# Three-pass products for two more layers of the first block, and the order of the splits around them

## The chip, the cores and the metric

One Trainium2 chip, one of its cores. The metric is the device time of one execution in microseconds (us); for the kernel before it is the median of three runs.

## What is computed

The reference has three parts in a row. The first is a linear attention with decay over 4 sequences of 768 steps with 8 heads of 48 columns (`state` is a 48x48 matrix for each sequence and head). The second is a feed-forward layer pair 384 -> 2048 -> 384 with a clipped gate, the third a gated pair 384 -> 1536 -> 384 behind a root-mean-square norm:

```
y[t]  = r[t] @ (state + (u * k[t]) (x) v[t]);  state = w[t] * state + k[t] (x) v[t]
h = x @ w_in;   x = (h * clip(h + 3, 0, 6) / 6) @ w_out
xn = x / rms(x) * rms_g;   out = (silu(xn @ w_gate) * (xn @ w_val)) @ w_out
```

All inputs and outputs are float32. The change lies in the second part, at its first block of tokens, and in the hand-over of attention output to the second block.

## The kernel before, in words

**Blocks and steps.** The 768 positions are cut into six blocks of 128 positions of all 4 sequences (512 tokens each). For each block c the second part runs over 16 tiles f of 128 hidden columns. One pass over a tile is a step; `steps` numbers them. Block 0 has its first five tiles cut in two halves of 256 tokens (steps 0 to 9), then whole tiles (step n has tile f = n - 5, steps 10 to 20). Block 1 is steps 21 to 36 (f = n - 21).

**What a step issues.** In this order: the list `before[n]`; `ff1` (first product of this tile into one of two PSUM buffers `hps`, then the clip on ACT, L466, and the product with h on DVE, L467, which frees that buffer); the list `between[n]`; `ff2` of the tile two steps earlier (the second product); the list `behind[n]`. After each step `pin` chains the instructions of every engine, so that each engine takes them in exactly the order of the program. An instruction that waits holds up all that stand behind it on its engine.

**Two ways to multiply.** For block 0 and f below `F32_F` the products are plain float32: `emit_h_f32` and `emit_out_f32` (L455, L461), six matrix products for a layer half. From `F32_F` on, and in all later blocks, each operand is a pair of parts, a high one (a rounded copy made on ACT) and a low one (the rest, made by a subtraction), and `emit_h` and `emit_out` (L449, L478) make three passes over three slices, nine products. The split of the activation is `emit_split`: high part on ACT (L471), low part on POOL (L472). The split of the block's tokens is `x_parts` for block 0 (L608 on ACT, L609 on DVE) and `Job.split` for later blocks (L425 on ACT, L426 on POOL).

**Weights.** A tile of the second part's weights comes as 64-bit words: `load` (L138, SP), `scale` (L146, ACT), `bits` (L151, L152, DVE), which puts them into a tile `x`, and from there a transfer (L155, SP) to their place in `wide_a` or `wide_b`. `parts` (L161 on ACT, L162 on DVE) turns that into the high and low part. Steps: for f below 12 `parts` runs two steps before block 1 needs the tile (f + 19); for f from 12 on, one step before block 0 does (f + 4).

**Attention.** Each job j (block j // 4, sequence j % 4) is laid out by `plan(j, n)` over six steps: `scans` (two scans, L280, DVE) and `bonus1` (L307, L308, POOL) at n; `muls` (L303, DVE), `bonus2` (L312, DVE, a sum over what `bonus1` made) and `decay` (POOL) at n + 1; `fill` (eight copies, L338, ACT), `pe_a` (L361), `pe_kt` (L345), `choose` (L367, DVE), `copy_kt` (L350, ACT) at n + 2; `pe_y` (L397, L403), `pe_u` (L376), `copy_y` (L409 on ACT, then eight transfers by SP, L412 to L415), `add_u` (L385, DVE) at n + 3; `split` at n + 5. Jobs 4 to 7 have n = 6, 9, 12, 15, jobs 8 and 9 have n = 19 and 23. So `pe_y` of job 7 is in step 18, its `split` in step 20, and `pe_y` of job 8 is in step 22. Block 1's first product, step 21, reads the split of job 7; `choose` writes over the tile that `fill` wrote and `pe_y` multiplies by it.

Of the kernel before, what the change touches and what calls it, by code (L numbers as in the profile page):

```python
# [9 lines left out]
F32 = mybir.dt.float32  # L10
# [3 lines left out]
AF = mybir.ActivationFunctionType  # L14
ALU = mybir.AluOpType
AX = mybir.AxisListType

B, H, S, D = 4, 8, 768, 48
# [5 lines left out]
KT = DM // 128  # L24
F1 = 2048 // 128
# [4 lines left out]
WP = 4 * DM  # L30
NG = F2 // 3
LAGS = (5, 0, 0, 0, 0, 0)
F32_F = 12


@with_exitstack
def kernel(
# [15 lines left out]
    nc = tc.nc  # L53
# [23 lines left out]
    x0 = st_p.tile([128, KT, TOK], F32, tag="x0", name="x0", bufs=1)  # L77
# [53 lines left out]

    class Weight:
        def __init__(self, src):
            self.src, self.near = src, False

        def load(self):
            self.raw = st_p.tile([128, 2 * DM], U64, tag="raw", name="raw", bufs=3)
# [11 lines left out]
        def bits(self):  # L149
            x = st_p.tile([128, 2 * DM], U32, tag="x", name="x", bufs=3)  # L150
            nc.vector.tensor_scalar(x, self.words()[0], 29, None, ALU.logical_shift_right)  # L151
            nc.vector.scalar_tensor_tensor(  # L152
                out=x, in0=self.mag.bitcast(U32), scalar=3, in1=x, op0=ALU.logical_shift_left, op1=ALU.bitwise_or)
            self.x = x.bitcast(F32).rearrange("p (a n) -> p a n", a=2)
            nc.sync.dma_start(  # L155
                out=self.dst[:, :, 1, :].bitcast(U32), in_=x.rearrange("p (a n) -> p a n", a=2))
            if not self.near:
                self.x = self.dst[:, :, 1, :].bitcast(F32)
# [103 lines left out]
    xts = {0: xt_p.tile([128, KT, 2, TOK], F32R, tag="xt", name="xt")}  # L262
# [196 lines left out]
    def emit_out_f32(acc, slot, g, first, cols):  # L459
        for m in range(KT):  # L460
            nc.tensor.matmul(  # L461
                acc[m][:, cols], slot[:, m * 128:(m + 1) * 128], g,
                start=first, stop=True, skip_group_check=not first)
# [5 lines left out]
    def emit_split(a, n, p=None):  # L469
        g = (p or rg_p).tile([128, 2, n], F32R, tag="g", name="g")  # L470
        nc.scalar.activation(out=g[:, 0, :], in_=a, func=AF.Copy)  # L471
        nc.gpsimd.tensor_tensor(out=g[:, 1, :], in0=a, in1=g[:, 0, :].bitcast(F32), op=ALU.subtract)  # L472
        return g
# [9 lines left out]
    def new_acc():  # L483
        return [ps_o.tile([128, TOK], F32, tag=f"o{m}", name=f"o{m}") for m in range(KT)]
# [51 lines left out]
    wa = [Weight(wa_d[f]) for f in range(F1)]  # L536
# [9 lines left out]
    before, between, behind = ([[] for _ in steps] for _ in range(3))  # L546

    def plan(j, n):

        jb = jobs[j]  # L550
        before[n] += [jb.scans, jb.bonus1]
        before[n + 1] += [jb.muls, jb.bonus2, jb.decay]
        before[n + 2] += [jb.fill]
        between[n + 2] += [jb.pe_a, jb.pe_kt, jb.choose, jb.copy_kt]
        between[n + 3] += [jb.pe_y, jb.pe_u, jb.copy_y, jb.add_u]
        if j + 2 < len(jobs):
            behind[n + 3] += [lambda: jobs[j + 2].load("w", "rk", "v")]
        if j + 1 < len(jobs):
            behind[n + 1] += [lambda: jobs[j + 1].load("rks")]
        (before if jb.b == B - 1 else behind)[n + 5] += [jb.split]  # L560


    j0, j1, j2, j3 = jobs[:B]
# [11 lines left out]
    for j, n in zip(range(B, 2 * B), (6, 9, 12, 15)):  # L575
        plan(j, n)
    for c in range(2, NC_):
        for b in range(B):
            plan(c * B + b, first[c] - 18 + 4 * b)
# [6 lines left out]
        if f + 3 < F1:  # L586
            behind[n] += [wa[f + 3].load]
    for f in range(F1):
        if f in (6, 10):
            behind[f + 19] += [wa[f].parts]  # L590
        else:
            before[f + 19 if f < F32_F else f + LAGS[0] - 1] += [wa[f].parts]
    behind[2] += [lambda: jobs[4].load("w", "rk", "rks", "v")]
    behind[4] += [lambda: jobs[5].load("w", "rk", "v")]

# [6 lines left out]
    for c in range(1, NC_):  # L602
        norm_plan(c, first[c], False)

    def x_parts():
        for k in range(KT):
            h = xts[0][:, k, 0, :]
            nc.scalar.activation(out=h, in_=x0[:, k, :], func=AF.Copy)  # L608
            nc.vector.tensor_tensor(out=xts[0][:, k, 1, :], in0=x0[:, k, :], in1=h.bitcast(F32), op=ALU.subtract)  # L609

    behind[F32_F + LAGS[0] - 2] += [x_parts]
    acc, norms, todo = None, {}, []


# [12 lines left out]
    def ff1(c, f, cols):  # L627
        n = cols.stop - cols.start
        ps = ps_h.tile([128, n], F32, tag="h", name="hps")
        if c == 0 and f < F32_F:  # L630
            if cols.start:
# [4 lines left out]
        else:  # L636
# [3 lines left out]
            g = emit_split(a, n)  # L640
        x = wa[f].x[:, 1] if c == 0 and f < F32_F else wpair[f][:, 1]
        todo.append((c, f, cols, g, x))

    def ff2(c, f, cols, g, x):
        nonlocal acc
        first, last = f == 0 and cols.start == 0, f == F1 - 1
        if first:
            acc = new_acc()
        if c == 0 and f < F32_F:
            emit_out_f32(acc, x, g, first, cols)  # L650
# [5 lines left out]
    def run(fs):  # L656
        for x in fs:
            x()
# [302 lines left out]
    for i in range(2):  # L961
        nc.sync.dma_start(
            out=uc[64 * i:64 * i + D, :, i], in_=u_d.rearrange("o (p i d) -> i d (o p)", p=NP, i=2)[i])
# [24 lines left out]
    for f in range(W1):  # L988
        wa[f].dst = wpair[f]
        wa[f].near = f < 2  # L990
    run((j0.scans, j0.pairs, j0.pe_bonus, j0.muls, j1.pairs, j0.fill, j0.pe_a, wa[0].scale, j1.pe_bonus, j1.fill))
    run((j1.scans, j1.muls, lambda: j1.pe_a(True), j0.choose, j0.pe_y0, wa[0].bits, wa[3].load, j1.choose, j1.pe_y0))
    run((wa[1].scale, wa[1].bits, wa[4].load, j2.pairs, j2.scans, j0.copy_y0, j1.copy_y0))
# [150 lines left out]
    for j in range(6 * NG + 1):  # L1144
        p, k = divmod(j, 2 * NG)
# [34 lines left out]
        want, n = {5: 7, 6: 6}.get(j, 9), 0  # L1180
# [107 lines left out]
```

## Time and profile before

| | |
|---|---|
| median of 3 runs | 944.44 us (943.24 to 944.67) |
| the profiled execution | 943.37 us, of it 941.6 us from the first to the last instruction |
| TensorE (PE) busy | 926.5 us, 98%, granted clock 1.0 |
| VectorE (DVE) busy | 645.5 us, 69% |
| ScalarE (ACT) busy | 475.6 us, 51% |
| GpSimd (POOL) busy | 532.8 us, 57% |

An engine's busy share is an average over stages. Times in the rows below count from the first instruction of the execution. A row of the timeline merges equal instructions that follow each other; ends of matrix products are modelled and overlap the next one, so that the length of a stretch on PE is read from start to start. The bracket at the end of a row is the idle time of the engine just before it, with what ended it.

### The profile page before, as it was taken

What the parts mean: (1) busy time and instruction counts of PE and PEld (TensorE: products, weight loads), DVE (VectorE), ACT (ScalarE), POOL (GpSimd) and SP (SyncE); (2) the same over time, 40 slices, a digit from 0 to 9 for tenths busy, and PEclk for the clock granted to TensorE, in tenths of its full rate; (3) what the DMA queues carried; (4) which work ended last, traced back from release to release, by engine and by line L of the source; (5) the groups of instructions that cost most, each with busy time, mean ns of one, the idle gap of its engine ahead of it and who ended that gap; (6) DMA issues with size and microseconds to landing.
All of it is one profiled execution on the core that took longest, in us unless ns stands there. A gap on an engine that the chain in (4) does not pass through costs nothing.

```text
span 941.6 us, 14286 instructions
## 1 busy us (share of the span) xinstructions
PE 926.5 (98%) x5085; PEld 733.1 (78%) x5085; DVE 645.5 (69%) x913; ACT 475.6 (51%) x946; POOL 532.8 (57%) x454
## 2 busy tenths in 40 slices
PE   5999999999999999999999999999999999999998
PEld 5775578888878887777888888887877778888886
DVE  7787767776868777677545377648988467555555
ACT  4554656656545555654554654445555445433331
POOL 0033355766846776675466676589466678335423
PEclk9999999999999999999999999999999999999999
DMA  8888532247445554642653387763699732644321
GB/s 338 310 302 297 191 138 84 92 165 246 167 145 198 170 184 156 228 163 58 242 193 112 125 310 262 279 244 141 226 381 325 272 154 92 243 168 155 147 79 68
DMA packets 63127, 184.77 MB, mean 196 GB/s; under 512 B 8912, under 2 KB 23248, under 8 KB 58448
## 3 DMA queue, kind: packets, MB, share of 16 engines
q1 hardware_dynamic: 63056, 183.87, 55.1%
q8 instruction: 40, 0.66, 0.3%
q14 instruction: 31, 0.25, 0.1%
HBM read 134.29 MB, written 39.32 MB: 184 GB/s over the span
## 4 chain that ended last, share of the span: by engine, by line
PE 92%; DMA 3%; DVE 2%; ACT 1%; issue 1%; POOL 1%; SPq 0%; POOLq 0%; ACTq 0%
PE o L478 19%; PE hps L449 18%; PE o L765 15%; PE pe L765 10%; PE pc L765 9%; PE pa L765 4%; PE o L461 3%; PE hps L455 3%; PE pb L765 3%; PE aps L361 2%; PE yps L403 2%; DMA raw<-in_dram 2%; PE pd L765 1%; PE yps L397 1%; PE ktp L345 1%; PE ups L376 1%
## 5 line engine op out<-in xcount | busy, mean ns | idle before, releaser
L472 POOL TENSOR_TENSOR g<-a,g 128x512 fp32r<-128x512 f32 x84 | 115.9, 1379 | 145.0 <-ACT g L471 132.8
L467 DVE SCALAR_TENSOR_TENSOR a<-a,hps 128x512 f32<-128x512 f32 x84 | 57.3, 682 | 94.6 <-ACT a L466 93.1
L478 PE MATMUL o<-g,wide_b 128*128 128x512 f32 x441 | 113.3, 399 | 0.0
L449 PE MATMUL hps<-xt,wide_b 128*128 128x512 f32 x441 | 111.9, 398 | 0.0
L765 PE MATMUL o<-xt,wide_b 128*128 128x512 f32 x405 | 107.7, 395 | 0.0
L466 ACT ACTIVATE a<-hps,half 128x512 f32<-128x512 f32 x84 | 57.5, 684 | 94.3 <-PE hps L449 89.9
L449 PEld LDWEIGHTS hps<-xt,wide_b 128*128 128x128 f32 x441 | 82.7, 188 | 21.2 <-issue 1.2
L478 PEld LDWEIGHTS o<-g,wide_b 128*128 128x128 f32 x441 | 81.2, 188 | 19.4 <-issue 0.5
L471 ACT ACTIVATE g<-a 128x512 fp32r<-128x512 f32 x84 | 53.1, 633 | 78.9 <-DVE a L467 76.8
L765 PEld LDWEIGHTS o<-xt,wide_b 128*128 128x128 f32 x405 | 76.0, 188 | 18.3
L478 PE MATMUL o<-g,wide_a 128*128 128x512 f32 x315 | 78.7, 394 | 0.0
L449 PE MATMUL hps<-xt,wide_a 128*128 128x512 f32 x315 | 77.6, 390 | 0.2 <-POOL xt L426 0.2
L280 DVE TENSOR_TENSOR_SCAN w<-w,dd 128x520 f32<-128x520 f32 x48 | 74.4, 1551 | 4.6 <-DMA w<-in_dram 2.8
L449 PEld LDWEIGHTS hps<-xt,wide_a 128*128 128x128 f32 x315 | 59.0, 188 | 13.3 <-POOL xt L426 0.6
L478 PEld LDWEIGHTS o<-g,wide_a 128*128 128x128 f32 x315 | 58.2, 188 | 12.3 <-issue 0.2
L800 DVE TENSOR_TENSOR q<-pc,q 128x512 f32<-128x512 f32 x80 | 55.1, 688 | 17.6 <-PE pc L765 6.7
L338 ACT ACTIVATE a<-iperm,cb 128x128 f32<-128x128 f32 x192 | 58.5, 388 | 0.1
L866 POOL TENSOR_TENSOR q<-q,q 128x512 f32<-128x512 f32 x36 | 49.2, 1367 | 13.5 <-DVE q L800 13.3
L765 PE MATMUL o<-g,wide_b 128*128 128x512 f32 (+1 forms) x216 | 55.5, 390 | 0.0
L862 ACT ACTIVATE q<-q 128x512 f32<-128x512 f32 x40 | 25.3, 633 | 48.6 <-DVE q L800 48.6
L800 DVE TENSOR_TENSOR q<-pe,q 128x512 f32<-128x512 f32 x40 | 27.5, 688 | 32.1 <-PE pe L765 32.1
L307 POOL TENSOR_TENSOR rks<-rks 128x384 f32<-128x384 f32 x20 | 31.1, 1556 | 30.6 <-DMA rks<-in_dram 30.6
(206 smaller groups left out, 2002.0 us busy)
## 6 DMA issues: line engine op xcount, KB each, us to landing
wraw<-in_dram SPq DMA_DIRECT2D x36, 384.0 KB, 4.0
wide_b<-wo SPq DMA_DIRECT2D x12, 1152.0 KB, 8.5
w<-wd SPq DMA_DIRECT2D x10, 1280.0 KB, 5.9
wide_b<-wd SPq DMA_DIRECT2D x10, 1280.0 KB, 6.1
w<-in_dram SPq DMA_DIRECT2D x24, 520.0 KB, 3.8
rk<-in_dram SPq DMA_DIRECT2D x24, 512.0 KB, 5.2
raw<-in_dram SPq DMA_DIRECT2D x16, 768.0 KB, 7.5
rks<-in_dram SPq DMA_DIRECT2D x20, 384.0 KB, 5.4
```

The costliest lines, as they stand in the source:

```text
L280: nc.vector.tensor_tensor_scan(out=x, data0=x, data1=dd.rearrange("p a h j -> p (a h j)"), initial=0.0, op0=ALU.mult, op1=ALU.add)
L307: nc.gpsimd.tensor_tensor(out=x, in0=x, in1=self.rks[:, 1, :], op=ALU.mult)
L338: nc.scalar.activation(out=self.head(h), in_=iperm, func=AF.Copy, scale=self.cb[:, h, :])
L449: nc.tensor.matmul(ps, slot[:, l, k * 128:(k + 1) * 128], xt[:, k, r, :], start=(k == 0 and j == 0), stop=(k == KT - 1 and j == 2))
L466: nc.scalar.activation(out=a, in_=ps, func=AF.Relu, scale=1.0 / 6.0, bias=half)
L467: nc.vector.scalar_tensor_tensor(out=a, in0=a, scalar=1.0, in1=ps, op0=ALU.min, op1=ALU.mult)
L471: nc.scalar.activation(out=g[:, 0, :], in_=a, func=AF.Copy)
L472: nc.gpsimd.tensor_tensor(out=g[:, 1, :], in0=a, in1=g[:, 0, :].bitcast(F32), op=ALU.subtract)
L478: nc.tensor.matmul(acc[m][:, cols], slot[:, l, m * 128:(m + 1) * 128], g[:, r, :], start=(first and j == 0), stop=(parts or last and j == ...
L765: nc.tensor.matmul(ps, lhs[:, l, :], rhs[:, r, :], start=first and j == 0, stop=True, skip_group_check=not (first and j == 0))
L800: nc.vector.tensor_tensor(out=out, in0=a, in1=b, op=op)
L866: eng.tensor_tensor(out=o, in0=src, in1=self.gate.o[i], op=ALU.mult)
```

## The change

Tiles 10 and 11 of block 0 go over to three passes (`F32_F` 12 to 10). Tiles 10 to 15 stay in the tile `x` until `parts` reads them; their transfer to `wide_b` (L155) is left out. `parts` of tiles 10 and 11 moves from steps 29 and 30 to the ends of steps 13 and 14; `parts` of tiles 12 to 15 keeps its step and moves to the front of that step's list. `x_parts` is cut in three, one slice at the end of steps 6, 7 and 8 in place of all three at the end of step 15, and its subtraction moves from DVE to POOL. `split` of job 7 moves from step 20 to step 19, ahead of job 8's `scans` and `bonus1` there.

```diff
-F32_F = 12
+F32_F = 10
...
             self.x = x.bitcast(F32).rearrange("p (a n) -> p a n", a=2)
+            if self.stays:
+                return
             nc.sync.dma_start(
...
-        (before if jb.b == B - 1 else behind)[n + 5] += [jb.split]
+        if j == 2 * B - 1:
+            before[n + 4] += [jb.split]
+        else:
+            (before if jb.b == B - 1 else behind)[n + 5] += [jb.split]
...
     for f in range(F1):
-        if f in (6, 10):
-            behind[f + 19] += [wa[f].parts]
+        if f < F32_F:
+            (behind if f in (6, 10) else before)[f + 19].append(wa[f].parts)
         else:
-            before[f + 19 if f < F32_F else f + LAGS[0] - 1] += [wa[f].parts]
+            if f < 12:
+                behind[f + 3] += [wa[f].parts]
+            else:
+                before[f + 4].insert(0, wa[f].parts)
...
-    def x_parts():
-        for k in range(KT):
-            h = xts[0][:, k, 0, :]
-            nc.scalar.activation(out=h, in_=x0[:, k, :], func=AF.Copy)
-            nc.vector.tensor_tensor(out=xts[0][:, k, 1, :], in0=x0[:, k, :], in1=h.bitcast(F32), op=ALU.subtract)
-
-    behind[F32_F + LAGS[0] - 2] += [x_parts]
+    def x_parts(k):
+        h = xts[0][:, k, 0, :]
+        nc.scalar.activation(out=h, in_=x0[:, k, :], func=AF.Copy)
+        nc.gpsimd.tensor_tensor(out=xts[0][:, k, 1, :], in0=x0[:, k, :], in1=h.bitcast(F32), op=ALU.subtract)
+
+    for k in range(KT):
+        behind[6 + k] += [lambda k=k: x_parts(k)]
...
+    for f in range(F32_F, F1):
+        wa[f].stays = True
```

## Rows read from the trace of the kernel before

**Rows 1.** Timeline of PE: start us, length us, engine, line, operation, tiles, count.

```profile
60.67 0.67 PE L397 MATMUL yps<-rk,st 64*64 64x128 f32 x16 [0.31 <-DVE a L367]
...
83.55 2.74 PE L461 MATMUL o<-g,wide_a 128*128 128x512 f32 x6
86.13 2.74 PE L455 MATMUL hps<-x,wide_b 128*128 128x512 f32 x6
...
114.06 0.67 PE L397 MATMUL yps<-rk,st 64*64 64x128 f32 x16
...
123.01 2.26 PE L449 MATMUL hps<-xt,wide_b 128*128 128x512 f32 x9
125.11 2.26 PE L478 MATMUL o<-g,wide_b 128*128 128x512 f32 x9
...
127.80 2.12 PE L449 MATMUL hps<-xt,wide_a 128*128 128x512 f32 x8 [0.20 <-POOL xt L426]
...
135.66 0.67 PE L397 MATMUL yps<-rk,st 64*64 64x128 f32 x16
```

**Rows 2.** Timeline of ACT: job 4's fill in step 8, and the token split.

```profile
56.02 2.44 ACT L338 ACTIVATE a<-iperm,cb 128x128 f32<-128x128 f32 x8
...
98.70 1.65 ACT L608 ACTIVATE xt<-x 128x512 fp32r<-128x512 f32 x3
```

**Rows 3.** Timeline of DVE, steps 14 to 22.

```profile
92.03 1.63 DVE L152 SCALAR_TENSOR_TENSOR x<-mag,x 128x768 uint32<-128x768 uint32 x1
...
93.73 1.24 DVE L280 TENSOR_TENSOR_SCAN w<-w,dd 128x520 f32<-128x520 f32 x1
...
101.16 1.29 DVE L303 TENSOR_TENSOR rk<-rk,w 128x512 f32<-128x512 f32 x2
...
102.83 0.95 DVE L162 TENSOR_TENSOR wide_b<-wide_b 128x768 fp32r<-128x768 f32 x1
...
109.23 1.34 DVE L367 COPY_PREDICATED a<-mask,aps 128x512 f32<-128x512 uint32 x2
...
111.78 1.65 DVE L152 SCALAR_TENSOR_TENSOR x<-mag,x 128x768 uint32<-128x768 uint32 x1
...
116.73 1.96 DVE L280 TENSOR_TENSOR_SCAN w<-w,dd 128x520 f32<-128x520 f32 x1
...
118.96 1.62 DVE L280 TENSOR_TENSOR_SCAN w<-w,dd 128x520 f32<-128x520 f32 x1
...
132.72 1.36 DVE L367 COPY_PREDICATED a<-mask,aps 128x512 f32<-128x512 uint32 x2
```

**Rows 4.** Timeline of POOL, step 19: job 8's `bonus1`.

```profile
117.55 1.94 POOL L307 TENSOR_TENSOR rks<-rks 128x384 f32<-128x384 f32 x1
119.57 1.83 POOL L308 TENSOR_TENSOR rks<-rks,ub 128x384 f32<-128x384 f32 x1
```

**Rows 5.** Timeline of ACT, steps 15 to 21.

```profile
97.40 0.60 ACT L409 ACTIVATE y<-yps 128x512 f32<-128x512 f32 x1 [0.98 <-PE yps L403]
...
103.74 0.91 ACT L146 ACTIVATE mag<-raw 128x768 f32<-128x768 f32 x1
...
107.81 0.69 ACT L466 ACTIVATE a<-hps,half 128x512 f32<-128x512 f32 x1
...
116.14 0.58 ACT L409 ACTIVATE y<-yps 128x512 f32<-128x512 f32 x1
...
124.25 0.51 ACT L425 ACTIVATE xt<-x 128x384 fp32r<-128x384 f32 x1
124.67 0.83 ACT L161 ACTIVATE wide_a<-wide_a 128x768 fp32r<-128x768 f32 x1
...
127.50 0.63 ACT L471 ACTIVATE g<-a 128x512 fp32r<-128x512 f32 x1 [1.43 <-DVE a L467]
```

**Rows 6.** Timeline of SP: the last four of job 7's eight output transfers.

```profile
119.28 2.49 SPq L415 DMA_DIRECT2D x<-y  x4
```

**Rows 7.** DMA issues from 90 to 130 us: count, KB each, median us to landing.

```profile
x<-y SPq DMA_DIRECT2D x4, 16.0 KB, 1.8
```

More of the change, by code (lines that the diff above doesn't have):

```diff
@@ L133, in __init__ @@
         def __init__(self, src):
-            self.src, self.near = src, False
+            self.src, self.near, self.stays = src, False, False
         def load(self):
```

## Prediction

> **What bounds the kernel now.** I read the table of engines first, then the list of waits of PE, then the timelines of PE, ACT, DVE, POOL and SP from step 6 to step 23. PE is busy almost throughout, and in the stretch that the change touches it waits twice: for `choose` of job 4 in step 9, and for the low part of job 7's tokens at the start of block 1 [rows 1]. So any time that PE loses here stays lost, and PE time saved counts whole, as long as ACT, DVE and POOL still deliver in time. They are not far ahead: what each timeline shows is one long alternation, in which ACT waits for DVE's product and DVE for ACT's clip.
>
> **The gain on PE.** A float32 half layer takes 2.58 us from start to start (83.55 to 86.13), a three-pass one 2.10 (123.01 to 125.11) [rows 1]. Four halves change over (`ff1` and `ff2` of tiles 10 and 11): 4 x 0.48 = -1.92 us. Three of them lie ahead of `pe_y` of job 7. Each of the two tiles adds a high part on ACT, 0.63 [rows 5], and a low part on POOL; six transfers of weights vanish, which no wait of PE hung on, so 0.
>
> **The token split, steps 6 to 8.** Three slices took 1.65 on ACT, 0.55 each [rows 2]. Slices 0 and 2 fall where ACT idles before the next clip: 0. Slice 1 comes directly ahead of job 4's `fill` [rows 2], behind which stand the clip of step 8, its product, `choose`, and then PE, which already waits 0.31 for it [rows 1]. I take +0.55, bounds 0 (if ACT found the room) and +0.61. The subtraction on POOL lies beside idle time of DVE: 0. In step 15, where `x_parts` was, ACT and DVE win room, which is used up below.
>
> **The late tiles, steps 14 to 18.** I follow the queue on the clock of before, moved by +0.55.
> - DVE is done with `bits` of tile 13 at 93.66 + 0.55 = 94.2 [rows 3]. `parts` of tile 11 is new there, 0.95 [rows 3]: 95.1.
> - `scans` of job 7: 2.8 if nothing slows them (two of 1.24 and the reciprocal), 3.85 if they run as those of job 8 (116.73 to 120.58), beside which POOL ran `bonus1` [rows 3, 4]. Job 7's `bonus1` lies beside all of them now; I take 3.85: 98.95. The product of tile 10 follows, 0.7: 99.65.
> - ACT then has the new high part (0.6), `copy_y` of job 6 and `scale` (97.40 to 98.70, 1.30), `parts` of tile 12 (0.83) [rows 2, 5]: 102.4. `parts` stands first in its step now, so DVE idles until then; it, `muls` and the sum took 101.16 to 103.78, 2.6 [rows 3], and the product 0.7: 105.7.
> - ACT: the second new high part (0.6), then `scale`, `parts`, `fill` of job 7 and the clip, which took 103.74 to 108.50, 4.75 [rows 5]: 111.05. Product and `choose` of job 7 took 108.50 to 110.57, 2.05 [rows 3, 5]: 113.1. PE reaches `pe_y` of job 7 at 114.06 + 0.55 - 3 x 0.48 = 113.2 [rows 1]. Just in time: 0, bounds 0 and 0.8.
> - Behind `choose`, `bits` of tile 15 takes till 2.86 later (110.57 to 113.43), then `parts` 0.95, the product 0.7, the high part 0.6 [rows 3, 5]: `copy_y` of job 7 would start at 118.2; as instructions in a row overlap by some 0.08, I take 117.8. If DVE kept pace it would follow `pe_y` by 2.08 as before (114.06 to 116.14) [rows 1, 5]: 115.25.
>
> **The split of job 7 a step sooner.** What it waits for does not come sooner. From `copy_y` at 116.14 to the landing of the last of eight transfers, which SP issues at 119.28 + 2.49 - 0.6 = 121.2, it is 1.8 more: 123.0, so 6.8 us [rows 5 to 7]. In step 20 ACT met it landed. In step 19 only `parts` of tile 15 stands between `copy_y` and the split, and ACT stands still some 6 us. Queued behind it: `parts` of tile 0, the clip of step 19, all of step 20, `fill` of job 8. Queued on POOL behind the low part: `bonus1` of job 8. Call the landing L = 117.8 + 6.8 = 124.6 (122.05 if DVE kept pace).
> - Split, `parts` and DVE's half of `parts` (0.42 + 0.83 + 0.95) and the product (0.7) [rows 3, 5]: `hps` of step 19 is free at L + 2.9 = 127.5. Step 21 needs that buffer; PE gets there at 125.11 + 2.10 + 0.55 - 1.92 = 125.84 [rows 1]. It waits 1.7, bounds 0 and 2.5. This takes the place of the 0.20 for POOL.
> - DVE: `muls`, then the sum, which needs `bonus1`. POOL has the low part and `bonus1` to do from L + 0.5; by the slow `bonus1` (117.55 to 121.40, 3.85) [rows 4] and a low part at that pace (some 1.75) the sum starts at L + 6.1; if POOL is quick it starts when DVE is through with the product and `muls` (2.9 + 1.2), at L + 4.1. I take L + 5.5, nearer to the slow row, since DVE's `parts` and `muls` run beside it. Sum, `parts` of tile 1, product: 2.1, so the high part of step 20 starts at L + 7.65.
> - From that high part (127.50) to the end of `choose` of job 8 (134.08) it took 6.6 [rows 3, 5], and all of that keeps its order: L + 14.25, PE 0.15 later: 139.0. PE began `pe_y` of job 8 at 135.66 [rows 1].
>
> **The sum** at `pe_y` of job 8: 139.0 - 135.66 = +3.3 us. It holds -1.92, +0.55, the wait at step 21 and one of about 3 at step 22. Behind it PE's list of waits holds next to nothing that could take it up. The profiled execution took 943.37, the median 944.44, 1.07 more; the change is added to the median: 947.7. Bounds: with L = 122.05 and the sum at L + 4.1 `pe_y` starts at 135.0, -0.6. With every DVE instruction slow, `choose` of job 7 late by 0.8 and L at 125.4, it is about +5.
>
> **Rivals.**
> 1. *DVE keeps pace* (for it: scans of 1.24 [rows 3]; in step 15 DVE loses `x_parts`). `copy_y` is prompt, no wait at step 21, a short one at step 22: 943.8 by the lower bound. That is within what a measurement can tell from no change (0.2%, 1.9 us). Against it: the two new high parts each put a wait for DVE into ACT's queue.
> 2. *Faster: ACT is not held.* Place: ACT's queue in step 19. Price: the 6.8 us. If the transfers have landed when ACT is through with `parts` of tile 15, all behind is done ahead of PE. From `pe_y` of job 7 to that of job 8 PE needs 21.6 - 0.48 - 0.4 = 20.7 [rows 1]; the chain needs at least 2.08 + 6.8 + 12.95 = 21.8, so it decides from 1.1 us sooner on. Then -1.92, -0.2 and, if step 8 has room too, no +0.55: 942.4. For it: only that the waits now sit in other queues. Against it: eight issues by SP cannot shrink.
> 3. *Slower still: DVE and POOL shut each other out.* Each DVE instruction beside a POOL one waits for the whole of it: some 0.9 more in `scans` of job 7, 0.75 in `parts` of tile 0, 0.8 in `muls` and `parts` of tile 1: +5.7, 950.1. The rows bear it out in part: a scan of 1.24 took 1.96 beside `bonus1`, which took 1.94 itself, so that both lost [rows 3, 4].
>
> The Trainium skill, SBUF — State Buffer, section "Who interferes with whom", states the third rival as a rule: a DVE instruction with two SBUF inputs and a POOL instruction share one pair of ports, and the later one blocks fully. By that rule the time would be near 950.1; by the rows, in which both ran on at a lower pace, it is the forecast's 947.7. The change adds two low parts and three slices to POOL, so the rule speaks against it.
>
> **How the numbers follow.** Forecast 0.60, rival 1 0.20, rival 2 0.10, rival 3 0.10. Slower by over 0.2%: 0.60 + 0.10 = 0.70; within: 0.20; faster: 0.10. The range leaves out rival 2 and the far half of rival 3: 943.7 (the lower bound and a little) to 949.9.
>
> **What would show it.** On PE, L455 and L461 gone from tiles 10 and 11; a wait of 0.7 to 0.9 for DVE at `pe_y` of job 4; a wait of PE at the first product of block 1 whose releaser is DVE's L467; one of 1 to 3.5 at `pe_y` of job 8, released by L367; on ACT an idle stretch of 5 to 6 us ahead of L425 in step 19, ended by DMA. It is wrong if ACT shows no such stretch, or if PE passes both places without a wait.

## The result, and the profile after

Median of six executions of the changed kernel: 950.93 us (949.07 to 3225.03); of the kernel before, beside it, 943.5 us (942.4 to 944.67). The ratio is 1.0069, interval [1.0055, 1.0083]: slower. Two executions took some 3225 us and are set aside in the ratio; nothing here explains them, and as the median counts them, it lies above the four others, 949.07, 949.09, 950.46 and 951.4, whose middle is 949.8. Run again (e8 below) the same kernel took 948.17, ratio 1.0055 [1.0043, 1.0068]. So the change costs between 4.7 us (948.17 against 943.45 beside it) and 6.3 us (949.8 against 943.5); 3.3 were forecast. The profiled execution is the longest of the four, 951.4 us with a span of 949.6, against 943.37 before: +8.0.

The engine table of the page after, PE and the others:

```profile
PE 928.0 (98%) x5097; PEld 737.9 (78%) x5097; DVE 645.5 (68%) x910; ACT 476.4 (50%) x948; POOL 542.2 (57%) x459
```

DVE's busy time is what it was, ACT has gained under 1 us, POOL 9.4. Shares of busy time say nothing of the loss. PE's list of waits does (engine and line that waited, what for; us in all, times, longest us):

```profile
PE cps L328 <- DVE rp L322: 9.1, 1, 9.1
PE yps L399 <- DVE a L369: 2.9, 3, 1.8
PE hps L451 <- DVE a L469: 2.6, 1, 2.6
PE pe L773 <- DMA w<-wd: 1.8, 1, 1.8
```

The first stands at the start of the kernel and was 8.7 before; in the ten profiles of this case it lies between 7.8 and 9.5, and the changed kernel itself has 7.9 in e8, so its length belongs to the execution and not to the change. The other three are new or have grown; on PE's timeline they look like this (start us, length us, engine, line, operation, count, in brackets the wait ahead of it; lines after are 2 higher than before around here, so L399 answers to L397 and L451 to L449 of [rows 1]):

```profile
61.53 0.67 PE L399 MATMUL yps<-rk,st 64*64 64x128 f32 x16 [0.81 <-DVE a L369]
...
113.48 0.67 PE L399 MATMUL yps<-rk,st 64*64 64x128 f32 x16
...
128.95 3.82 PE L451 MATMUL hps<-xt,wide_a 128*128 128x512 f32 x9 [2.64 <-DVE a L469]
132.70 1.16 PE L363 MATMUL aps<-rk 48*128 48x128 f32 x16
...
140.41 0.67 PE L399 MATMUL yps<-rk,st 64*64 64x128 f32 x16 [1.83 <-DVE a L369]
...
705.44 1.45 PE L773 MATMUL pe<-wide_b,w 128*128 128x512 f32 x3 [1.79 <-DMA w<-wd]
```

Read against [rows 1], `pe_y` of job 4 begins 0.86 later (0.50 of it the longer wait, 0.36 the start of the kernel), that of job 7 0.58 sooner, that of job 8 4.75 later. The whole loss of the first stage is made in these 27 us, and the 2.64 stand where [rows 1] have 0.20. The nine products behind them take 3.75 (128.95 to 132.70), where such a row takes 2.10 [rows 1]. The table by stretches says why (the stretch and its length, then PE, PEld, DVE, ACT, POOL busy, granted clock of PE, share of the DMA engines, GB/s):

```profile
120.00:128.00 8.00, 6.31 (x28) 4.73 (x26) 4.07 (x6) 1.83 (x3) 1.52 (x2) 1.00 0.34 102
128.00:133.00 5.00, 4.05 (x13) 3.03 (x15) 5.00 (x6) 1.94 (x3) 4.92 (x4) 0.66 0.44 161
133.00:137.00 4.00, 4.00 (x32) 3.40 (x29) 0.68 (x2) 3.29 (x10) 2.08 (x4) 1.00 0.96 338
```

ACT is busy for 1.83 of 8 us ahead of it, and behind PE's wait the granted clock is 0.66 on average, so part of the stretch at 1.2 GHz and the rest at 2.4 GHz. ACT's timeline, step 18 to 20, answers to [rows 5]:

```profile
117.69 0.63 ACT L473 ACTIVATE g<-a 128x512 fp32r<-128x512 f32 x1 [2.75 <-DVE a L469]
118.22 0.58 ACT L411 ACTIVATE y<-yps 128x512 f32<-128x512 f32 x1
118.70 0.84 ACT L163 ACTIVATE wide_b<-x 128x768 fp32r<-128x768 f32 x1
125.88 0.52 ACT L427 ACTIVATE xt<-x 128x384 fp32r<-128x384 f32 x1 [6.34 <-DMA x<-y]
126.31 0.83 ACT L163 ACTIVATE wide_a<-wide_a 128x768 fp32r<-128x768 f32 x1
...
133.72 0.63 ACT L473 ACTIVATE g<-a 128x512 fp32r<-128x512 f32 x1 [2.85 <-DVE a L469]
```

`copy_y` of job 7 (L411) begins 4.74 after `pe_y`, where it was 2.08 [rows 1, 5], since ACT stands in front of it waiting for DVE's product. Then ACT stands 6.34 ahead of the split, waiting for its transfers. Those are issued by SP, whose last four answer to [rows 6]:

```profile
121.30 3.35 SPq L417 DMA_DIRECT2D x<-y  x4
```

DVE behind the split, with `parts` of tile 11 and the scans of job 7 first, and POOL beside it ([rows 3, 4]):

```profile
94.46 1.77 DVE L164 TENSOR_TENSOR wide_b<-x,wide_b 128x768 fp32r<-128x768 f32 x1
...
96.29 1.91 DVE L282 TENSOR_TENSOR_SCAN w<-w,dd 128x520 f32<-128x520 f32 x1
...
98.47 1.24 DVE L282 TENSOR_TENSOR_SCAN w<-w,dd 128x520 f32<-128x520 f32 x1
...
127.17 1.12 DVE L164 TENSOR_TENSOR wide_a<-wide_a 128x768 fp32r<-128x768 f32 x1 [3.82 <-ACT wide_a L163]
128.22 0.68 DVE L469 SCALAR_TENSOR_TENSOR a<-a,hps 128x512 f32<-128x512 f32 x1
128.82 2.31 DVE L305 TENSOR_TENSOR rk<-rk,w 128x512 f32<-128x512 f32 x2
131.05 0.54 DVE L314 TENSOR_REDUCE cb<-rks 128x8 f32<-128x384 f32 x1
...
138.93 1.33 DVE L369 COPY_PREDICATED a<-mask,aps 128x512 f32<-128x512 uint32 x2
```

```profile
127.44 1.71 POOL L309 TENSOR_TENSOR rks<-rks 128x384 f32<-128x384 f32 x1
129.23 1.35 POOL L310 TENSOR_TENSOR rks<-rks,ub 128x384 f32<-128x384 f32 x1
130.53 1.73 POOL L474 TENSOR_TENSOR g<-a,g 128x512 fp32r<-128x512 f32 x1
```

The product at 128.22 frees the `hps` buffer on which PE waited; `choose` at 138.93 is what `pe_y` of job 8 waited for.

### The profile page after: what moved, and what is told of

Read it like the earlier page. It is cut to its first block, busy times and chain, and to the rows that moved or that the text cites. A ratio compares the mean times of both kernels' runs of the same rounds, so it can differ in the third digit from the quotient of the medians.

```text
span 949.6 us, 14296 instructions
## 1 busy us (share of the span) xinstructions
PE 928.0 (98%) x5097; PEld 737.9 (78%) x5097; DVE 645.5 (68%) x910; ACT 476.4 (50%) x948; POOL 542.2 (57%) x459
## 4 chain that ended last, share of the span: by engine, by line
PE 89%; DVE 4%; DMA 3%; ACT 2%; issue 1%; SPq 0%; DVEq 0%
PE o L480 19%; PE hps L451 18%; PE o L773 14%; PE pe L773 9%; PE pc L773 8%; PE pa L773 4%; PE pb L773 3%; PE o L463 2%; PE hps L457 2%; PE aps L363 2%; PE yps L405 2%; PE pd L773 1%; PE yps L399 1%; DMA w<-wd 1%; PE ups L378 1%; ACT a L340 1%
## 5 line engine op out<-in xcount | busy, mean ns | idle before, releaser
L474 POOL TENSOR_TENSOR g<-a,g 128x512 fp32r<-128x512 f32 x86 | 118.7, 1381 | 140.2 <-ACT g L473 140.1
L480 PE MATMUL o<-g,wide_b 128*128 128x512 f32 x459 | 118.0, 400 | 0.0
L451 PE MATMUL hps<-xt,wide_b 128*128 128x512 f32 x459 | 116.4, 397 | 0.0
L451 PEld LDWEIGHTS hps<-xt,wide_b 128*128 128x128 f32 x459 | 86.1, 187 | 22.0 <-issue 1.2
L480 PEld LDWEIGHTS o<-g,wide_b 128*128 128x128 f32 x459 | 84.4, 188 | 20.2 <-issue 0.5
L451 PE MATMUL hps<-xt,wide_a 128*128 128x512 f32 x315 | 78.9, 396 | 2.6 <-DVE a L469 2.6
L451 PEld LDWEIGHTS hps<-xt,wide_a 128*128 128x128 f32 x315 | 60.2, 191 | 16.1 <-DVE a L469 3.1
L773 PEld LDWEIGHTS o<-g,wide_b 128*128 128x128 f32 x216 | 40.2, 188 | 9.5
```

What stands on the lines that cost most here:

```text
L451: nc.tensor.matmul(ps, slot[:, l, k * 128:(k + 1) * 128], xt[:, k, r, :], start=(k == 0 and j == 0), stop=(k == KT - 1 and j == 2))
L480: nc.tensor.matmul(acc[m][:, cols], slot[:, l, m * 128:(m + 1) * 128], g[:, r, :], start=(first and j == 0), stop=(parts or last and j == ...
L773: nc.tensor.matmul(ps, lhs[:, l, :], rhs[:, r, :], start=first and j == 0, stop=True, skip_group_check=not (first and j == 0))
```

## The experiments

Theory A is that of the forecast: ACT, held in step 19 by a split whose transfers have not landed, makes the loss. Theory B, its rival: the late tiles' parts put ACT and DVE into arrears from step 14 on, `copy_y` of job 7 is late by itself, and the loss comes wherever the tokens of block 1 are asked for. All runs are measured beside the kernel before (943.42 and 943.45 in the two sessions). Diffs are against the changed kernel unless said otherwise.

**e1: the split of job 7 back in step 20.**

```diff
-        if j == 2 * B - 1:
-            before[n + 4] += [jb.split]
-        else:
-            (before if jb.b == B - 1 else behind)[n + 5] += [jb.split]
+        (before if jb.b == B - 1 else behind)[n + 5] += [jb.split]
```

> The changed kernel with the split of job 7 back in step 20, all else kept. Theory A (the split holds ACT in step 19, and that costs most): ACT shows no idle stretch for a transfer ahead of L427, PE does not wait for L369 at pe_y of job 8, and the time is 942 to 943.5 us. Theory B (the two new three-pass tiles put ACT and DVE late by themselves): the hold is gone, yet PE waits 2 to 4 us at the first product of block 1, now for POOL's low part of job 7 (L428); 945 to 946.5 us, and 1.7 more if the granted clock falls to half behind that wait as it did in the changed kernel.

Measured: 947.08 us (945.01 to 947.68), 1.0038 [1.0024, 1.0052]. ACT is not held any more, and PE waits at the same place, now for the low part of the tokens. Its timeline, and the stretch behind that wait:

```profile
128.45 3.33 PE L451 MATMUL hps<-xt,wide_a 128*128 128x512 f32 x8 [2.33 <-POOL xt L428]
131.70 1.49 PE L363 MATMUL aps<-rk 48*128 48x128 f32 x16
```

```profile
129.00:133.00 4.00, 4.00 (x23) 2.94 (x21) 1.09 (x2) 3.56 (x10) 1.51 (x3) 0.57 0.78 283
```

At `pe_y` of job 8 it does not wait. The eight products take 3.25 from start to start; e5 below, at full clock, has the same eight in 2.04. With 0.33 more in `pe_a` (1.49 against 1.16) the half clock costs 1.5 here, and nothing covers it. So a loss of 3.7 us (947.08 against 943.42) is there without the hold: B's mechanism exists. The profiled execution is the shortest of the five, 945.01; what the longer ones lost beyond it stands in no trace.

**e2: `F32_F` 12 again, the rest as changed.**

```diff
-F32_F = 10
+F32_F = 12
```

> The changed kernel with F32_F back at 12: tiles 10 and 11 stay float32, the split of job 7 stays in step 19, the token slices stay in steps 6 to 8. Theory A: ACT idles 5 to 6 us ahead of the split, PE waits 2.5 to 3.5 us for L369 at pe_y of job 8 (little or nothing at the first product of block 1), 946.5 to 948 us. Theory B: without the two tiles ACT and DVE keep pace, PE waits less than 1 us at either place, 943.5 to 945 us.

Measured: 947.42 us (945.33 to 948.16), 1.0038 [1.0023, 1.0053]. Without the two added tiles `copy_y` of job 7 follows `pe_y` by 2.08 (115.52 to 117.60), as in the kernel before, and block 1 starts without a wait. But ACT is held, and PE pays at `pe_y` of job 8. ACT's and PE's timelines:

```profile
124.47 0.53 ACT L427 ACTIVATE xt<-x 128x384 fp32r<-128x384 f32 x1 [5.56 <-DMA x<-y]
```

```profile
139.06 0.67 PE L399 MATMUL yps<-rk,st 64*64 64x128 f32 x16 [2.36 <-DVE a L369]
139.66 1.88 PE L405 MATMUL yps<-a,v 128*64 128x128 f32 x16
```

`pe_y` begins 14.59 after the landing, in the changed kernel 14.53 (125.88 to 140.41). That is A's mechanism, alone. e1 loses 3.7 us and e2 4.0, but e1 has the 1.92 that PE gains by the two tiles and e2 has not. Without that gain e1 loses 5.6, e2 4.0 and the changed kernel 6.6 to 8.2, less than the 9.6 of the two together: both hang on the same chain, so that they don't add up.

**e3: e1, and the parts of tiles 12 to 15 at the end of their step's list.**

```diff
-                before[f + 4].insert(0, wa[f].parts)
+                before[f + 4].append(wa[f].parts)
```

> The changed kernel with the split of job 7 back in step 20 and the parts of tiles 12 to 15 back at the end of their steps' lists. If standing first is what makes DVE idle until ACT is through (theory B's place), copy_y of job 7 comes 1 to 2 us sooner than with the parts first and PE waits at most 1 us at the first product of block 1, 943 to 944 us; PE may wait some 1 us in step 20 for the parts of tile 15. If the order in the list does not matter, it is like the first experiment.

Measured: 944.38 us (942.29 to 945.64), 1.0010 [1.0001, 1.0019]. PE's timeline has two short waits in place of one long one, and the granted clock stays 1.00:

```profile
123.58 1.90 PE L451 MATMUL hps<-xt,wide_b 128*128 128x512 f32 x7 [1.23 <-DVE wide_b L164]
...
128.23 2.12 PE L451 MATMUL hps<-xt,wide_a 128*128 128x512 f32 x8 [0.42 <-POOL xt L428]
```

`copy_y` of job 7 did not come sooner, against the expectation (3.77 after `pe_y`, 3.68 in e1), so the arrears are not cured by this order. They fall into two places, and the clock is not lost: 2.7 us less than e1.

**e4: the kernel before, with the token split alone moved to steps 6 to 8, its subtraction on POOL.** The diff is the `x_parts` part of the change, with nothing else of it.

> The kernel before with only the token split moved to steps 6 to 8 and its subtraction to POOL. By the prediction's step: the wait of PE at pe_y of job 4 grows from 0.31 to 0.8 to 0.9 us, no other wait changes, +0.5 us. By its rival (ACT finds the room) the wait stays at 0.3, and the 1.9 us that DVE wins in step 15 change nothing either.

One execution: 945.02 us. PE's waits:

```profile
PE yps L397 <- DVE a L367: 0.8, 1, 0.8
```

0.31 has become 0.8 [rows 1], and nothing else that PE waits for behind the kernel's start has changed. The step is worth +0.5, on the path. This execution is 1.65 longer than the profiled one of before; the other 1.15 stand ahead of that wait (`pe_y` of job 4 begins at 62.32, before at 60.67), and from there to `pe_y` of job 8 the two kernels agree (75.03 and 74.99).

**e5: e1, with the low parts of tiles 12 and 15 on POOL and the token slices in steps 6, 8 and 9.**

```diff
-            nc.vector.tensor_tensor(
+            (nc.gpsimd if self in (wa[12], wa[15]) else nc.vector).tensor_tensor(
...
-        behind[6 + k] += [lambda k=k: x_parts(k)]
+        behind[(6, 8, 9)[k]] += [lambda k=k: x_parts(k)]
```

> The changed kernel with the split of job 7 back in step 20, the low parts of tiles 12 and 15 subtracted on POOL in place of DVE, and the token slices in steps 6, 8 and 9 (none ahead of job 4's fill). If what is left after the split is put back is DVE that idles for parts standing first (theory B), copy_y of job 7 comes within 2.3 us of pe_y as in the kernel before, PE waits at most 1 us at the first product of block 1, 0.3 at pe_y of job 4, the granted clock stays full: 941.5 to 942.8 us. If the backlog is ACT's (two more high parts), it stays as in the first experiment, 945 to 946.5.

Measured: 943.65 us (942.4 to 945.17), 1.0002 [0.9993, 1.0011]: about 1 us above the expectation. `copy_y` of job 7 follows `pe_y` by 3.00 (114.19 to 117.19), where 2.3 were expected, so part of the arrears is still there. What is left is a wait at full clock, and in the profiled execution, the longest of the eleven, one of 1.4 for `w<-wd` near 700 us:

```profile
128.56 2.11 PE L451 MATMUL hps<-xt,wide_a 128*128 128x512 f32 x8 [1.32 <-POOL xt L428]
```

`pe_y` of job 4 waits 0.30, as before the change: moving slice 1 out of step 7 gives the 0.5 back.

**e6: job 7's split in step 19 behind job 8's `bonus1`, both halves on POOL, so that ACT isn't held.**

```diff
-            nc.scalar.activation(out=xt[:, :, 0, :], in_=x, func=AF.Copy)
+            if self.i == 2 * B - 1:
+                nc.gpsimd.tensor_copy(xt[:, :, 0, :], x)
+            else:
+                nc.scalar.activation(out=xt[:, :, 0, :], in_=x, func=AF.Copy)
...
-        if j == 2 * B - 1:
-            before[n + 4] += [jb.split]
-        else:
+        if j != 2 * B - 1:
...
+    before[19] += [jobs[2 * B - 1].split]
```

> The changed kernel, but both halves of job 7's split run on POOL, still in step 19, behind bonus1 of job 8: the wait for the transfers stays, on another engine's queue. If it is the hold on ACT that costs (theory A), PE's wait at the first product of block 1 falls from 2.6 to 1 to 1.5 us and changes its releaser to POOL, the one at pe_y of job 8 stays at 1.5 to 2.5 because DVE and ACT are late by themselves: 945 to 947 us. If any engine's hold costs the same, 949 to 951.

Measured: 946.19 us (944.98 to 948.32), 1.0030 [1.0019, 1.0042]. The time is as expected, the waits are not: block 1 starts with hardly a wait (0.18), where 1 to 1.5 were expected, but `copy_y` is late as ever (4.31 after `pe_y`), and so is all of the chain to `choose` of job 8:

```profile
138.41 0.67 PE L399 MATMUL yps<-rk,st 64*64 64x128 f32 x16 [2.81 <-DVE a L369]
```

Taking the hold away from ACT and leaving the arrears moves the wait and does not remove it.

**e7: e5 and e6 together, and `scale` of tile 8 one step later.** Beside the edits of both:

```diff
-            (behind[n - 1] if n else before[n]).append(wa[f].scale)
+            (behind[n if f == 8 else n - 1] if n else before[n]).append(wa[f].scale)
```

> The two experiments above in one (low parts of tiles 12 and 15 on POOL, slices in steps 6, 8, 9, split of job 7 on POOL in step 19 behind bonus1), and scale of tile 8 behind step 8's clip, so that nothing but fill stands ahead of job 4's choose. If A and B are the whole loss, PE waits less than 0.3 us at each of the four places (pe_y of job 4, first product of block 1, pe_y of jobs 7 and 8), the granted clock stays full and the gain of 1.9 us on PE comes through: 941.0 to 942.0 us. If something else keeps the tokens late, 942.5 to 944.

Measured: 941.48 us (940.26 to 942.18), 0.9978 [0.9970, 0.9987], 2.0 less than the kernel before (943.45) and 6.7 less than the changed one in the same session. In this stretch PE waits once, and passes `pe_y` of job 8 without a stop (less than 0.3 at every place was expected):

```profile
126.02 2.11 PE L454 MATMUL hps<-xt,wide_a 128*128 128x512 f32 x8 [0.71 <-POOL xt L431]
...
133.91 0.67 PE L399 MATMUL yps<-rk,st 64*64 64x128 f32 x16
```

`copy_y` of job 7 follows `pe_y` by 3.01, as in e5: the arrears are smaller than the 4.74 of the changed kernel and not gone (2.08 before). Of the 2.2 us between e5 and e7, this stretch makes 0.6 and the wait at `pe_y` of job 4, which e7 does not have, 0.3; the rest lies outside of it.

**e8: the changed kernel again,** unaltered, to see whether the wait at 705 us belongs to the change.

> The changed kernel again, unaltered. In the first profile the granted clock fell to half twice, at 129 us behind PE's wait for DVE and at 706 us behind a wait for a weight transfer. If the second belongs to the change, every execution has a mean clock of 0.996 and takes 950 to 951.5 us; if it is an execution's own, some have 0.998 and take 949 to 949.5.

Measured: 948.17 us (947.66 to 950.27). PE's timeline repeats the two waits of the first stage:

```profile
128.41 3.52 PE L451 MATMUL hps<-xt,wide_a 128*128 128x512 f32 x9 [2.39 <-DVE a L469]
131.86 1.52 PE L363 MATMUL aps<-rk 48*128 48x128 f32 x16
...
139.86 0.67 PE L399 MATMUL yps<-rk,st 64*64 64x128 f32 x16 [1.76 <-DVE a L369]
```

Near 700 us it waits 0.9, for DVE's `planes`, not 1.79 for `w<-wd`. The fall at 705 is that execution's own, not a fixed part of the change: in the first session two of the four executions have a mean clock of 0.996 and two 0.998, here all five have 0.998. One of these five took 950.27 all the same, and nothing here says why.

**All of them in one measure.** From `pe_y` of job 7 to that of job 8 the start of the kernel plays no part. PE itself needs 21.40 there in the kernel before (135.66 - 114.06, less the wait of 0.20 [rows 1]), and 20.92 where the second product of tile 11, which lies in this stretch, is three-pass (0.48 less). What a kernel takes beyond that should be its waits and the time at half clock:

| kernel | interval, us | beyond PE's need | waits there | half clock there |
|---|---|---|---|---|
| before | 21.60 | 0.20 | 0.20 | none |
| changed | 26.93 | 6.01 | 2.64 + 1.83 | 1.65 |
| e8 | 26.67 | 5.75 | 2.39 + 1.76 | 1.71 |
| e1 | 24.83 | 3.91 | 2.33 | 1.54 |
| e2 | 23.54 | 2.14 | 2.36 | behind it |
| e3 | 22.82 | 1.90 | 1.23 + 0.42 | none |
| e5 | 22.26 | 1.34 | 1.32 | none |
| e6 | 23.83 | 2.91 | 2.81 | behind it |
| e7 | 21.65 | 0.73 | 0.71 | none |

The sums agree within 0.25 everywhere. "Half clock" is what the products and `pe_a` behind the wait took beyond their usual time. In the changed kernel it is covered: `choose` of job 8 hangs on the landing, and PE, slower by 1.65, waits so much less for it (1.83 in place of some 3.5). In e1, where `pe_y` of job 8 waits for nothing, it counts. In e2 and e6 it comes behind `pe_y`: from the second row of `pe_y` (139.66 and 139.01) to the next `ff1` 5.24 and 5.19 go by, 3.68 before, so 1.5 to 1.6 more.

## Why the prediction was right or wrong

The sign, the mechanism and its places came as forecast, the size did not: 3.3 us forecast, 4.7 to 6.3 measured, at the upper end of the range or beyond it. The step that failed is the landing of job 7's transfers: the sum put it 6.8 us behind `copy_y`, and it came 7.66 and 7.84 behind in the two profiled executions. Beside it the sum put two things at nothing: what the granted clock costs behind a wait, 1.5 to 1.7 us each time, and what comes behind `pe_y` of job 8, where the profiled execution loses another 3.3 at 705 us by a wait and the clock. Step by step, without the 0.36 of the late start:

- **PE's gain** was right: from `pe_y` of job 4 to that of job 7 it is 53.39 before [rows 1] and 51.95 after, -1.44, three times 0.48.
- **The token slice** was right: +0.55 forecast, +0.50 measured (0.31 to 0.81), and +0.5 alone in e4.
- **The late tiles**: `choose` of job 7 just in time, as forecast (no wait at 113.48). `copy_y` 4.74 behind `pe_y`, forecast 4.6 (4.31 in e8). This is luck in part, since two errors on the way nearly cancel: `parts` of tile 11 took 1.77 beside POOL's `bonus1`, 0.95 forecast, and the scans 3.42 (96.29 to 99.71), 3.85 forecast.
- **The landing was mis-sized**: "6.8 us" from `copy_y`, measured 7.66 (118.22 to 125.88). It is SP's last four issues, 3.35 in place of 2.49 [rows 6], and 3.53 in e8; e3 has 2.70, e1, e2, e5, e6 and e7 have 2.48 or 2.49, and there the landing came after 6.87 in e2 and 6.84 in e6, as forecast. In the two long sets one single issue takes 1.44 and 1.63, the others 0.59, and these two sets alone among job 7's have a transfer of the instruction queue beside them (`q8 instruction` in the list of DMA queues, 0.02 MB). e3's set has a smaller one (`q14`), the other sets have none; job 6's in e3 has both and took 3.54. So the lengthening goes with such a transfer. Whether that makes it was not tested, and why it falls there in the changed kernel stays open. I had taken the one value of the kernel before without a bound.
- **The wait at step 21** was forecast as 1.7 with bounds 0 and 2.5, and is 2.64, beyond the bound: 0.86 more from the landing, 0.06 from `copy_y` and 0.17 from what stands between landing and product (L + 3.07 in place of L + 2.9), less the 0.11 by which PE itself came later than reckoned.
- **Behind the landing** the steps held: the sum began at L + 5.17 (forecast 5.5), the high part of step 20 at L + 7.84 (7.65), `pe_y` of job 8 at L + 14.53 (14.4). The sum was 0.33 sooner and what follows it took 2.67 in place of 2.1, so here too errors cancel.
- **At `pe_y` of job 8** this gives +4.75 in place of +3.34: 0.36 late start, 0.86 landing, 0.14 `copy_y`, 0.13 behind it, less 0.08 for PE's earlier arrival at job 7. The wait there was forecast as about 3 and is 1.83, because PE lost 1.65 to its clock on the way.
- **"Behind it PE's list of waits holds next to nothing that could take it up"** was right for what could win time back, and said nothing of what could lose more. At the product that began at 180.82 before PE is 5.08 late (0.33 more), keeps this to 690 us, and then, in the profiled execution, waits 1.79 for a load and runs on at half clock; the product on DVE that began at 700.80 before comes 8.66 later. e8 does not have that fall and comes to +4.7.
- **What the working lacked** is the clock. It counted a wait of PE as its length alone. Here two long waits lie so close that the second covers what the clock costs behind the first, so this did not make the miss at 129 us, which is luck; it did make part of the one at 705 (1.5 beside the wait of 1.79: the products from 705.44 on take 5.11, the same ones in e8 3.57), and it makes 1.5 of e1's loss.

Rival 1 fell: the scans took 1.91 and 1.24, and `copy_y` was late. Rival 2 fell by ACT's 6.34. In it the 0.4 taken off PE's 21.6 should be the 0.20 of [rows 1], which makes its need 20.9; its time does not hang on that. Rival 3's time, 950.1, is nearest to some of the executions, but not by its reckoning: it has the sum later than forecast, and it came sooner.

Its mechanism is there, though, and the prediction's reading of it as a lower pace of both was wrong. `muls` took 2.31 beside POOL, against 1.29 [rows 3]. The second of its two multiplications ended at 131.13, 0.55 behind the end of POOL's L310 (130.58). POOL's L474, begun at 130.53, ended 1.13 behind that, and DVE's `parts` of tile 1, begun at 131.51, 0.82 behind L474. Undisturbed they take some 0.65, 1.29 and 0.95, so that each did nearly all its work behind the end of the other: they went by turns. The Trainium skill, SBUF — State Buffer, section "Who interferes with whom", says that a DVE instruction with two SBUF inputs contends with a POOL instruction that reads SBUF, and that the ports they share are an exclusive lock. The trace agrees in these three rows. What the turns cost was priced too high by the rival and about right by the forecast.

Not tried: the six dropped weight transfers by themselves, and why PE waits near 700 us in some executions (1.79, 1.4 and 1.1 us for a load in the changed kernel, e5 and e6, 0.9 and 0.8 for DVE's `planes` in e8 and e3) and not in others.

## What to carry to other kernels

An instruction moved ahead of what it waits for does not get its data sooner; it holds its engine's whole queue, and the engine to hold is one whose queue has nothing that the bound engine needs. e6 gave the wait to POOL and left the arrears, and still lost 2.7 us; e5 made the arrears smaller and had no hold, and took the time of the kernel before; e7, with both, gained 2.0. Where steps are removed from the bound engine, look first at the engines that feed it: 1.92 us of PE's work bought two more high parts, and a `copy_y` that came 2.7 us later behind `pe_y`. Waits of PE of up to 1.32 us cost about their length here (e3, e5, e7), one of 2.33 its length and a stretch at half clock besides (e1).

## What the runs showed of the hardware

PE's granted clock fell from 2.4 to 1.2 GHz behind single waits in a kernel in which PE is busy 98% of the time: behind 2.64, 2.39, 2.33, 2.36 and 2.81 us (changed, e8, e1, e2, e6), and behind the 1.79 at 705 (0.71 granted from 704 to 708 us); not behind 1.83 and 1.76 at `pe_y` of job 8 (changed, e8), 1.32 in e5, or 1.23 and 0.42 in e3. So the length of a wait alone did not decide it. What follows the wait took 1.5 to 1.7 us more than at full clock in each of the six cases. The Trainium skill, TensorE: Matmul & The Clock Gate, Part 1, states that the half clock is the idle state and that activity lifts it; the trace agrees, and the waits listed show that this comes to bear even in the middle of dense work.

A DVE instruction with two SBUF inputs and a POOL instruction went by turns in the three rows named above. One of SP's issues took 1.44 and 1.63 us in place of 0.59 where a transfer of the instruction queue lay beside it (changed, e8).
